# Attention weights divided by one engine per batch: GpSimd for the first, VectorE for the second

## The chip, the cores and the metric

The kernel runs on one core of one Trainium2 chip. The metric is the device time of one launch in microseconds (us). A profile records one execution: every instruction of the five engines, with its start and length, and the DMA transfers. The engines are called here as the profile calls them or by name: PE is TensorE (matrix products; PEld its loading of weights), DVE is VectorE, ACT is ScalarE, POOL is GpSimd, and SP issues DMAs.

## The reference

Attention over a narrow window feeds two gated blocks. Cut to what matters here:

```python
# q, k, v: (2 batches, 8 heads, 768 positions, 64); n_global 8, n_local 96
scores = scale * q @ k.T + bias             # bias falls with the distance
scores = where(is_global | is_local, scores, -1e9)
a = exp(scores - max(scores, -1))
a = a / (sum(a, -1) + 1e-9)                 # the division that the change is about
x = a @ v                                   # -> (2, 768, 512)
x = (sigmoid(conv5(x)) * (x @ w_val)) @ w_out
h = relu(x @ w_in)
out = (h * sigmoid(conv3(h))) @ w_out2
```

## The kernel before

**Tiles.** A batch of 768 positions is six tiles of 128; the twelve tiles are numbered t = 0 to 11, so 0 to 5 are the first batch. Since the window is narrow, a tile of queries meets only its own tile of keys and the one before it: its scores are 128x256 for each of the eight heads (128x128 in tiles 0 and 6, the first of a batch).

**A tile in `fast_attention`.** It goes in two halves of four heads. TensorE makes the scores (L461). For each head VectorE adds the bias and finds the row's extreme in one custom instruction (`least`, L472, reads the scores from PSUM), and ScalarE takes the exponential and its row sum (`grow`, L477). When four heads are there, GpSimd adds 1e-9 to the four sums (`guard`, L488) and VectorE takes the reciprocals (`invert`, L491). Then each head's weights are multiplied by its reciprocal, in place in SBUF: this is the division. `on_dve` (L498) does it on VectorE, `on_pool` (L501) on GpSimd. TensorE then transposes two heads at a time (L528), ScalarE or VectorE copies the result out of PSUM (L532, L538), and TensorE multiplies it with the values (L553). The weights stand in a ring of 11 buffers `p`.

**Beside it.** The weight matrices come in units of 128x512 as 64-bit numbers, and each unit is made into float32 by ScalarE (L262), GpSimd (L264) and twice VectorE (L269, L272: a pair). `w_out` and `w_in` are multiplied with one another beforehand: 32 products of 128x512 on TensorE (L319), whose results VectorE and ScalarE split into two parts `W` (L236, L234). The taps of the convolutions are VectorE's (L671), with a first one on ScalarE or GpSimd (L666, L667). After this the kernel is a long row of TensorE products in three passes (L243 to L245); the first of them, the "values" of the first half of batch 0 with the matrix `w_val` (`wv` in the rows), need all four units of `wv`.

**The order.** Nothing is scheduled while the chip runs except by each engine's own queue, which is worked off in order. A planner (`Plan`) lays out all steps when the kernel is built: each step has an engine, an estimated cost and what it depends on, and the planner emits them by the resulting order. A step with two ways (`POOL=` or `DVE=` beside its engine) goes to the engine that would finish it first by the planner's estimates; so did the divisions.

Of the kernel before, what the change touches and what calls it, by code (L numbers as in the profile page):

```python
# [36 lines left out]
BIG = NEG * 2.0 ** NH * 1.01  # L37
QKSCALE = 1.0 / math.sqrt(D)
XPAIRS = 2
RAWS, MBUFS, HBUFS, Z2BUFS, PBUFS, PTBUFS, KQBUFS, VBUFS = 3, 2, 6, 3, 11, 4, 3, 4  # L40
EARLY = -5.0
LANDING = 2.4
# [40 lines left out]
class Plan:  # L83

    LAG = {"PE": 0.2, "ACT": 0.15, "DVE": 0.15, "POOL": 0.15, "SP": 0.0}
    START = {"DVE": 0.4, "ACT": 1.2, "SP": 0.3}
# [122 lines left out]
def act_us(n, sbuf=True, scaled=False, sums=False):  # L211
    return 0.05 + 0.000834 * n + 0.042 * sbuf + 0.092 * scaled + 0.093 * sums


def dve_us(n, scaled=False):
    return 0.069 + 0.001042 * n + 0.061 * scaled
# [6 lines left out]
def pool_us(n):  # L223
    return 0.17 + 0.0013 * n
# [27 lines left out]
def to_f32(c, dst, raw, n, bufs, reads, token):  # L252
# [5 lines left out]
    def whole(): return high().bitcast(F32)  # L258
    def bits(): return dst().bitcast(I32)
# [3 lines left out]
    pl.add(  # L263
        "POOL", pool_us(n), lambda: nc.gpsimd.tensor_scalar(whole(), whole(), 0.0, 1.0, ALU.mult, ALU.mult),  # L264
        bufs, reads + [token], [tail],
# [113 lines left out]
def head_ways(c, n, out, d, h):  # L379

    nc, k = c.nc, -slope(h) / QKSCALE
    return {
        "POOL": (0.02 + pool_us(n), lambda: nc.gpsimd.tensor_scalar(out(), d, k, 1.0, ALU.mult, ALU.mult)),
        "ACT": (act_us(n), lambda: nc.scalar.activation(out(), d, AF.Copy, scale=k)),
# [24 lines left out]
def fast_attention(c, ap):  # L409

    nc, ident, pl = c.nc, c.ident, c.plan
# [29 lines left out]
    def held(d, ts):  # L441
        return [d[t] for t in ts if t in d]

    for t in range(nt):
# [4 lines left out]
        nk = len(js) * P  # L449
        st, p = sts.new(), {}  # L450
        load(t)
        for half in range(2):
# [40 lines left out]
            four = [("p", t, h) for h in range(4 * half, 4 * half + 4)]  # L493
            pl.add("POOL", 0.12, guard, [st], four, [("r", t, half)])
            pl.add("DVE", 0.2, invert, [st], [], [("r", t, half)])
            for h in range(4 * half, 4 * half + 4):
                def on_dve(h=h, st=st, w=p[h], nk=nk):
                    nc.vector.tensor_scalar(w.t[:, :nk], w.t[:, :nk], st.t[:, 2, h : h + 1], None, ALU.mult)  # L498

                def on_pool(h=h, st=st, w=p[h], nk=nk):  # L500
                    nc.gpsimd.tensor_scalar(w.t[:, :nk], w.t[:, :nk], st.t[:, 2, h : h + 1], 1.0, ALU.mult, ALU.mult)  # L501

                pl.add(
                    "DVE", 0.13 + 0.00052 * nk, on_dve, [p[h], st], [("r", t, half)], [("p", t, h)],
                    POOL=(0.1 + pool_us(nk), on_pool),
                )

        def first_keys(t=t, i=i):
            r = (c.first[0] if t == 0 else kq[t].t)[:, :, 0, 0:GW]
# [3 lines left out]
        if i == 0:  # L513
            pl.add("POOL", 0.4, first_keys, held(kq, [t]), [("kq", t)], ["gl"])
        elif i < NT - 1:
            pl.add("POOL", 0.4, first_keys, held(kq, [t]), ["gl"], [("kq", t)])

        xp = c.ring["x"].new()
        pts = {}
        for pr in range(NPAIR):  # L520
# [15 lines left out]
            def by_dve(pt=pt, w=pts[pr], nw=len(js)):  # L536
# [5 lines left out]
                DVE=(dve_us(2 * nk), by_dve),  # L542
            )

            if pr % XPAIRS < XPAIRS - 1:
                continue

            def output(prs=range(pr - XPAIRS + 1, pr + 1), pts=pts, xp=xp, js=js):
                o = xp.t.rearrange("p (a q) -> p a q", q=P)
                for pr in prs:  # L550
                    for n, j in enumerate(js):
                        for z in range(2):
                            nc.tensor.matmul(  # L553
                                o[z * D : (z + 1) * D, pr, :], vals(j, 2 * pr + z), pts[pr].t[:, z, n, :],
                                start=n == 0, stop=n == len(js) - 1,
                            )

            prs = range(pr - XPAIRS + 1, pr + 1)
            pl.add(
                "PE", 0.213 * len(js) * XPAIRS, output, [xp] + [pts[q] for q in prs] + held(vs, js),  # L560
                [("pts", t, q) for q in prs] + [("v", j) for j in js], [("xp", t, q) for q in prs], mode="x",
            )
        if 0 < i < NT - 1:
# [10 lines left out]
            DVE=(  # L574
                dve_us(512),
                lambda xp=xp, i=i: nc.vector.tensor_copy(
                    c.x[:, :, XP + i * P : XP + (i + 1) * P], xp.t.rearrange("p (a q) -> p a q", q=P)
                ),
            ),
# [252 lines left out]
def attention_gated_mlps(ctx, tc, kq, v, nn, w_val, conv_w, w_out, w_in2, w_out2, out):  # L832
# [41 lines left out]
    def arm(fast):  # L874
        with ExitStack() as es:
# [42 lines left out]
            if fast:  # L918
                masks(c, ap)
                attention = fast_attention(c, ap)  # L920
                next(attention)
                n0 = len(pl.work)
# [78 lines left out]
```

## Time and profile before

| | |
|---|---|
| median of 3 runs | 289.19 us (288.85 to 289.6) |
| the profiled execution | 289.12 us |
| its span, first to last instruction | 286.9 us |
| mean granted TensorE clock | 0.998 |
| busy: PE, DVE, ACT, POOL | 94%, 83%, 65%, 33% |

The span is 2.2 us shorter than the time that the execution itself took. Busy shares are means over the whole span; they say little of a kernel that has stages with different limits, so the rows further below are taken by stretch. The lengths of instructions that follow one another on an engine overlap by some 0.08 us in the records, so what an instruction costs its queue is its record less that overlap (net).

### The profile page before, as it was taken

What the parts mean: (1) busy time and instruction counts of PE and PEld (TensorE: products, weight loads), DVE (VectorE), ACT (ScalarE), POOL (GpSimd) and SP (SyncE); (2) the same over time, 40 slices, a digit from 0 to 9 for tenths busy, and PEclk for the clock granted to TensorE, in tenths of its full rate; (3) what the DMA queues carried; (4) which work ended last, traced back from release to release, by engine and by line L of the source; (5) the groups of instructions that cost most, each with busy time, mean ns of one, the idle gap of its engine ahead of it and who ended that gap; (6) DMA issues with size and microseconds to landing.
All of it is one profiled execution on the core that took longest, in us unless ns stands there. A gap on an engine that the chain in (4) does not pass through costs nothing.

```text
span 286.9 us, 5416 instructions
## 1 busy us (share of the span) xinstructions
PE 270.1 (94%) x1832; PEld 227.9 (79%) x1832; DVE 238.6 (83%) x607; ACT 187.2 (65%) x468; POOL 95.4 (33%) x208
## 2 busy tenths in 40 slices
PE   2689799999999999999999999999999999999993
PEld 2567556564557998999999999988999988899882
DVE  3899999999999999999899999999985654356600
ACT  2899798967677879775688554894464354445510
POOL 4555557445554405563443310320512000003000
PEclk9999999999999999999999999999999999999999
DMA  4985756645634111023510000010000011000112
GB/s 133 344 322 143 239 197 213 251 138 169 216 108 148 48 65 58 9 75 93 170 43 0 2 0 0 1 39 38 37 2 0 0 73 39 37 0 2 39 73 85
DMA packets 10276, 26.17 MB, mean 91 GB/s; under 512 B 1408, under 2 KB 2688, under 8 KB 10240
## 3 DMA queue, kind: packets, MB, share of 16 engines
q1 hardware_dynamic: 9440, 25.22, 26.3%
q10 hardware_dynamic: 800, 0.52, 0.6%
q8 instruction: 16, 0.26, 0.4%
q14 instruction: 20, 0.16, 0.2%
HBM read 22.59 MB, written 3.15 MB: 90 GB/s over the span
## 4 chain that ended last, share of the span: by engine, by line
PE 73%; DVE 15%; POOL 3%; issue 3%; ACT 3%; POOLq 1%; DVEq 0%; ACTq 0%
PE s L244 8%; PE s L245 8%; PE s L243 8%; PE f L243 7%; PE f L245 7%; PE f L244 7%; PE s L461 4%; PE x L553 4%; PE t L528 4%; DVE p L472 3%; DVE z L671 2%; PE t L243 2%; PE t L245 2%; PE x L245 2%; PE x L244 2%
## 5 line engine op out<-in xcount | busy, mean ns | idle before, releaser
L477 ACT ACTIVATE p<-p,st 128x256 f32<-128x256 f32 (+1 forms) x96 | 46.1, 483 | 8.0 <-DVE st L472 6.4
L671 DVE SCALAR_TENSOR_TENSOR z<-h,cw,z 128x384 f32<-128x384 f32 x64 | 39.9, 630 | 12.6 <-ACT z L666 10.9
L673 ACT ACTIVATE z<-z 128x384 f32<-128x384 f32 (+2 forms) x48 | 25.2, 524 | 26.2 <-DVE z L671 25.5
L671 DVE SCALAR_TENSOR_TENSOR z<-x,cw,z 128x400 f32<-128x400 f32 (+1 forms) x64 | 39.6, 643 | 0.2
L244 PE MATMUL s<-w,g 128*128 128x512 f32 (+1 forms) x104 | 39.2, 377 | 0.0
L245 PE MATMUL s<-w,g 128*128 128x512 f32 (+1 forms) x104 | 39.2, 377 | 0.0
L243 PE MATMUL s<-w,g 128*128 128x512 f32 (+1 forms) x104 | 39.1, 376 | 0.0
L501 POOL TENSOR_SCALAR p<-p,st 128x256 f32<-128x256 f32 (+1 forms) x50 | 32.5, 660 | 11.0 <-DVE st L491 8.7
L528 PEld LDWEIGHTS t<-ident,p 128*128 128x128 f32 x176 | 19.8, 141 | 16.6 <-issue 5.0
L528 PE MATMUL t<-ident,p 128*128 128x128 f32 x176 | 28.7, 282 | 4.1 <-ACT pts L532 2.1
L319 PE MATMUL f<-w,w 128*128 128x512 f32 x64 | 30.8, 602 | 0.0
L472 DVE CUSTOM_DVE_ANT_0 p<-s,B 128x256 f32<-128x256 f32 x80 | 30.5, 410 | 0.0
L243 PE MATMUL f<-gg,Wh 128*128 128x400 f32 (+1 forms) x80 | 27.7, 347 | 0.0
L245 PE MATMUL f<-gg,Wl 128*128 128x400 f32 (+1 forms) x80 | 27.0, 338 | 0.0
L244 PE MATMUL f<-gg,Wh 128*128 128x400 f32 (+1 forms) x80 | 27.0, 338 | 0.0
L461 PE MATMUL s<-kq 64*128 64x128 f32 x320 | 25.7, 292 | 0.8 <-DVE st L472 0.7
L461 PEld LDWEIGHTS s<-kq 64*128 64x128 f32 x320 | 21.5, 194 | 4.9 <-issue 2.6
L667 POOL TENSOR_SCALAR z<-h,cw 128x384 f32<-128x384 f32 x10 | 8.9, 887 | 45.9 <-DVE z L671 31.0
L264 POOL TENSOR_SCALAR raw<-raw 128x512 f32<-128x512 f32 x24 | 18.3, 764 | 16.7 <-ACT m L262 14.1
L236 DVE TENSOR_TENSOR g<-z,g 128x384 fp32r<-128x384 f32 x32 | 17.8, 562 | 5.9 <-ACT g L234 5.9
L245 PEld LDWEIGHTS s<-w,g 128*128 128x128 f32 x104 | 19.5, 188 | 3.8
L244 PEld LDWEIGHTS s<-w,g 128*128 128x128 f32 x104 | 19.6, 188 | 2.8
(117 smaller groups left out, 633.6 us busy)
## 6 DMA issues: line engine op xcount, KB each, us to landing
raw<-in_moe_w_out_dram SPq DMA_DIRECT2D x12, 512.0 KB, 3.4
kq<-in_kq_dram SPq DMA_DIRECT2D x11, 512.0 KB, 4.4
raw<-in_moe_w_in_dram SPq DMA_DIRECT2D x8, 512.0 KB, 5.3
v<-in_v_dram SPq DMA_DIRECT2D x11, 256.0 KB, 3.6
out_dram<-o SPq DMA_DIRECT2D x11, 256.0 KB, 2.0
raw<-in_moe_w_val_dram SPq DMA_DIRECT2D x4, 512.0 KB, 3.5
v<-in_v_dram SPq DMA_DIRECT2D x8, 64.0 KB, 2.8
x<-in_kq_dram ACTq DMA_DIRECT2D x1, 256.0 KB, 4.0
```

The source lines that it names most:

```text
L243: nc.tensor.matmul(out, lh, rh, start=first, stop=False)
L244: nc.tensor.matmul(out, lh, rl, start=False, stop=False)
L245: nc.tensor.matmul(out, ll, rh, start=False, stop=last)
L264: "POOL", pool_us(n), lambda: nc.gpsimd.tensor_scalar(whole(), whole(), 0.0, 1.0, ALU.mult, ALU.mult),
L319: nc.tensor.matmul(ps.t, big["wot"].t.bitcast(F32)[:, e, cs], big[wi].t.bitcast(F32)[:, e, :], start=e == 0, stop=e == 3)
L461: nc.tensor.matmul(out, keys(t0, pr, 1)[hs], keys(j, pr, 0)[hs], start=True, stop=True)
L472: nc.vector.tensor_tensor_reduce(w.t[:, :nk], sc, bias, -QKSCALE, 3.0e38, ALU.add, ALU.min, st.t[:, 0, h : h + 1])
L477: nc.scalar.activation(w.t[:, :nk], w.t[:, :nk], AF.Exp, bias=st.t[:, 0, h : h + 1], scale=-1.0, accum_out=st.t[:, 1, h : h + 1],)
L501: nc.gpsimd.tensor_scalar(w.t[:, :nk], w.t[:, :nk], st.t[:, 2, h : h + 1], 1.0, ALU.mult, ALU.mult)
L528: nc.tensor.transpose(o[:, z, n, :], p[2 * pr + z].t[:, n * P : (n + 1) * P], ident)
L671: nc.vector.scalar_tensor_tensor(z(), src(k), w()[:, k : k + 1], z(), ALU.mult, ALU.add)
L673: pl.add("ACT", act_us(n), lambda: nc.scalar.activation(z(), z(), AF.Tanh, scale=0.5), bufs, [], [token])
```

## The change

In the first batch (t below `SHARED` = 6) every division is GpSimd's, in the second every one VectorE's; before, the planner placed each by itself. The planner's estimate for GpSimd differs a little from before.

```diff
+SHARED = 6
...
-                pl.add(
-                    "DVE", 0.13 + 0.00052 * nk, on_dve, [p[h], st], [("r", t, half)], [("p", t, h)],
-                    POOL=(0.1 + pool_us(nk), on_pool),
-                )
+                e, us, fn = ("POOL", 0.25 + 0.00094 * nk, on_pool) if t < SHARED else ("DVE", 0.13 + 0.00052 * nk, on_dve)
+                pl.add(e, us, fn, [p[h], st], [("r", t, half)], [("p", t, h)])
```

In the program before, VectorE had 27 of the first batch's 48 divisions and 19 of the second's; GpSimd had 21 and 29. Since the planner lays everything out anew, other steps move too: of the copies out of PSUM VectorE has 14 in place of 19 (L538, L576), and GpSimd makes 12 first taps in place of 18 (L667), ScalarE the rest. Lines above 502 are one lower in the changed kernel, lines from 40 to 500 one higher.

GpSimd's queue in the first batch, around tile 1, before. `st_325` holds the sums of tile 1, `p_` are buffers of weights, L488 is `guard`, L501 the division, L264 a unit of a weight matrix, L511 a copy of the global keys:

```order
L488 TENSOR_SCALAR st_325<-st_325 128x4
L501 TENSOR_SCALAR p_324<-p_324,st_325 128x256
L501 TENSOR_SCALAR p_347<-p_347,st_325 128x256
L264 TENSOR_SCALAR raw_330<-raw_330 128x512
L488 TENSOR_SCALAR st_325<-st_325 128x4
L511 TENSOR_SCALAR kq_305<-gl_225 128x4x32
L264 TENSOR_SCALAR cwr_226<-cwr_226 128x44
L501 TENSOR_SCALAR p_355<-p_355,st_325 128x256
```

The same place now, where `st_318` holds the sums of tile 1:

```order
L489 TENSOR_SCALAR st_318<-st_318 128x4
L502 TENSOR_SCALAR p_335<-p_335,st_318 128x256
L502 TENSOR_SCALAR p_317<-p_317,st_318 128x256
L502 TENSOR_SCALAR p_344<-p_344,st_318 128x256
L502 TENSOR_SCALAR p_339<-p_339,st_318 128x256
L489 TENSOR_SCALAR st_318<-st_318 128x4
L510 TENSOR_SCALAR kq_305<-gl_225 128x4x32
L265 TENSOR_SCALAR raw_270<-raw_270 128x512
L502 TENSOR_SCALAR p_357<-p_357,st_318 128x256
L502 TENSOR_SCALAR p_350<-p_350,st_318 128x256
L502 TENSOR_SCALAR p_388<-p_388,st_318 128x256
L502 TENSOR_SCALAR p_363<-p_363,st_318 128x256
```

Tile 1 had three divisions here and has eight, and the second `guard` stands behind the first four of them. Up to the last reciprocal of tile 5 GpSimd's queue has 42 divisions in place of 19 (8 of 128 columns and 34 of 256, for 4 and 15), 6 units of weight matrices in place of 9, and 2 first taps in place of 3.

VectorE's queue in the first batch, behind a reciprocal of tile 4 (`st_621`), before; `st_754` and `p_772`, `p_788` belong to tile 5, and the second L472 of each pair only writes out the extreme:

```order
L491 RECIPROCAL st_621<-st_621 128x4
L472 ISA p_772,st_754<-s_710,B_223 128x256
L472 ISA st_754 128x1
L498 TENSOR_SCALAR p_727<-p_727,st_621 128x256
L472 ISA p_788,st_754<-s_709,B_223 128x256
L472 ISA st_754 128x1
L498 TENSOR_SCALAR p_749<-p_749,st_621 128x256
L272 SCALAR_TENSOR_TENSOR w8_637<-w8_637,raw_680 128x4x128
```

Now, behind the same reciprocal (`st_612`; tile 5 has `st_761`):

```order
L492 RECIPROCAL st_612<-st_612 128x4
L473 ISA p_760,st_761<-s_732,B_223 128x256
L473 ISA st_761 128x1
L473 ISA p_772,st_761<-s_733,B_223 128x256
L473 ISA st_761 128x1
L473 ISA p_777,st_761<-s_732,B_223 128x256
L473 ISA st_761 128x1
L473 ISA p_780,st_761<-s_733,B_223 128x256
```

The divisions between the score instructions are gone. Up to the last reciprocal of tile 5 VectorE's queue loses 25 divisions (21 of 256 columns, 4 of 128), three L269, two L272 and two taps, and gets two copies out of PSUM of 512 columns, one of tile 1's output and one multiple of the mask more; the L269, L272 and taps now stand behind it. From there to the last unit of `wv` that VectorE finishes there are now 11 divisions of 256 columns and 8 of 128, where there were 3 and 4, also two score instructions of 256 columns and one of 128 more, and two copies of 256 columns less. ScalarE's queue up to tile 5's last exponential has 69 steps in place of 79.

TensorE's queue where the products of the two weight matrices begin (L319), before:

```order
L461 MATMUL s<-kq 128x128 x8
L319 MATMUL f<-w_328,w_637 128x512
L528 MATMUL t<-ident,p 128x128 x4
L319 MATMUL f<-w_328,w_637 128x512 x2
L528 MATMUL t<-ident,p 128x128 x4
L319 MATMUL f<-w_328,w_637 128x512
L553 MATMUL x<-pts,v 64x128 x16
```

Now:

```order
L552 MATMUL x<-pts,v 64x128 x8
L527 MATMUL t<-ident,p 128x128 x4
L320 MATMUL f<-w_415,w_748 128x512 x2
L527 MATMUL t<-ident,p 128x128 x4
L320 MATMUL f<-w_415,w_748 128x512 x2
L527 MATMUL t<-ident,p 128x128 x4
L552 MATMUL x<-pts,v 64x128 x8
```

They began between the transposes of tile 3 and now begin between those of tiles 4 and 5. Behind the second transposes of tile 5 (two heads, four blocks) stand 28 of the 32 products, where there were 22, and one half of tile 4's output product. Between that place and the first product with `wv` there are further the second half of the scores of tile 9 and one more group of four transposes, of tile 8; before, these stood behind the first product with `wv`.

## Rows read from the trace of the kernel before

**Rows 1.** The page's busy time, share of the span, instructions of each engine.

```profile
PE 270.1 (94%) x1832; PEld 227.9 (79%) x1832; DVE 238.6 (83%) x607; ACT 187.2 (65%) x468; POOL 95.4 (33%) x208
```

**Rows 2.** Busy us of PE, PEld, DVE, ACT, POOL in three stretches; then clock, DMA.

```profile
8.70:51.80 43.10, 39.18 (x368) 28.78 (x368) 41.93 (x160) 38.14 (x121) 25.05 (x51) 1.00 0.73 245
51.80:90.80 39.00, 37.63 (x256) 22.00 (x256) 38.61 (x101) 28.32 (x77) 20.88 (x31) 1.00 0.53 172
93.40:282.00 188.60, 188.60 (x1158) 173.08 (x1156) 151.10 (x315) 114.67 (x253) 45.85 (x109) 1.00 0.11 37
```

**Rows 3.** The chain that ended last: start us, us, what; each matmul recorded twice.

```profile
39.39 1.72 PE f L319 x4
...
95.78 0.44 PE t L528 x4
...
104.05 1.09 PE s L461 x16
105.14 1.02 PE x L553 x16
```

**Rows 4.** VectorE's timeline: start us, us, instruction.

```profile
16.84 0.34 DVE L498 TENSOR_SCALAR p<-p,st 128x256 f32<-128x256 f32 x1
...
51.85 0.17 DVE L491 RECIPROCAL st<-st 128x4 f32<-128x4 f32 x1
...
90.16 0.68 DVE L236 TENSOR_TENSOR wvl<-m,wvh 128x512 fp32r<-128x512 f32 x1
```

**Rows 5.** TensorE's timeline.

```profile
55.99 0.60 PE L528 MATMUL t<-ident,p 128*128 128x128 f32 x4
...
93.36 0.43 PE L243 MATMUL f<-gx,wvh 128*128 128x400 f32 x1
```

**Rows 6.** GpSimd by line, 9 to 52 us: busy us, mean ns; idle before.

```profile
L501 POOL TENSOR_SCALAR p<-p,st 128x256 f32<-128x256 f32 x15 | 8.2, 556 | 4.0 <-DVE st L491 3.8
L264 POOL TENSOR_SCALAR raw<-raw 128x512 f32<-128x512 f32 x9 | 6.5, 725 | 2.0 <-ACT w L262 1.9
L488 POOL TENSOR_SCALAR st<-st 128x4 f32<-128x4 f32 x11 | 3.4, 312 | 3.9 <-ACT p L477 3.3
L667 POOL TENSOR_SCALAR z<-x,cw 128x400 f32<-128x400 f32 x3 | 2.6, 888 | 1.3 <-ACT x L570 1.2
L501 POOL TENSOR_SCALAR p<-p,st 128x128 f32<-128x128 f32 x4 | 1.6, 396 | 0.3 <-PE s L461 0.3
L511 POOL TENSOR_SCALAR kq<-gl 128x128 f32<-128x128 f32 x4 | 1.2, 299 | 5.1 <-PE s L461 3.9 <-issue 1.1
```

**Rows 7.** The same, 52 to 91 us.

```profile
L501 POOL TENSOR_SCALAR p<-p,st 128x256 f32<-128x256 f32 x13 | 11.5, 901 | 1.7 <-DVE st L491 1.7
```

**Rows 8.** VectorE by line, 9 to 52 us.

```profile
L498 DVE TENSOR_SCALAR p<-p,st 128x256 f32<-128x256 f32 x21 | 9.7, 478 | 0.0
L269 DVE SCALAR_TENSOR_TENSOR raw<-raw 128x512 int32<-128x512 int32 x9 | 6.1, 680 | 0.0
L272 DVE SCALAR_TENSOR_TENSOR w<-w,raw 128x512 int32<-128x512 int32 x8 | 5.7, 712 | 0.1
L671 DVE SCALAR_TENSOR_TENSOR z<-x,cw,z 128x400 f32<-128x400 f32 x4 | 2.5, 613 | 0.0
L498 DVE TENSOR_SCALAR p<-p,st 128x128 f32<-128x128 f32 x4 | 1.1, 311 | 0.0
```

**Rows 9.** The same, 52 to 91 us.

```profile
L671 DVE SCALAR_TENSOR_TENSOR z<-x,cw,z 128x400 f32<-128x400 f32 x13 | 9.4, 730 | 0.0
L272 DVE SCALAR_TENSOR_TENSOR m<-m,raw 128x512 int32<-128x512 int32 x4 | 3.6, 889 | 0.1
```

**Rows 10.** GpSimd's timeline: one division, and four in a row.

```profile
29.22 0.48 POOL L501 TENSOR_SCALAR p<-p,st 128x256 f32<-128x256 f32 x1 [0.73 <-DVE st L491]
...
83.70 4.96 POOL L501 TENSOR_SCALAR p<-p,st 128x256 f32<-128x256 f32 x4 [0.38 <-DVE st L491]
```

**Rows 11.** The page's costliest groups: GpSimd's divisions over the whole span.

```profile
L501 POOL TENSOR_SCALAR p<-p,st 128x256 f32<-128x256 f32 (+1 forms) x50 | 32.5, 660 | 11.0 <-DVE st L491 8.7
```

## The prediction

> **What bounds the kernel now.** I read the page's busy shares first, then the busy time by stretch, then the chain that ended last. TensorE is busy 94% of the span [rows 1], but that is a mean over two stages. From 93.4 us to 282 us it is busy for all of 188.6 us [rows 2], and the chain runs along it: this stage lasts as long as TensorE's products do, and what VectorE or GpSimd gain within it buys nothing by itself. It can only begin earlier or hold less work. It begins at 93.36 us with the first product with `wv` [rows 5]. Ahead of it, from 8.7 us to 90.8 us, the fullest engine is VectorE: 41.9 of 43.1 us and 38.6 of 39.0 us [rows 2]. VectorE's last subtraction of a unit of `wv` begins at 90.16 us and ends 0.68 us later [rows 4]. So the question is when VectorE and TensorE reach that point. TensorE's own queue is not slack either: it is busy 37.6 of 39.0 us in the second stretch.
>
> I split the first stage at the last reciprocal of tile 5, which VectorE starts at 51.85 us [rows 4]; most of the first batch's attention is then behind it.
>
> **First stretch, VectorE.** A division of 256 columns on VectorE costs its queue 0.26 us undisturbed (0.34 less the overlap of 0.08, [rows 4]), but in this stretch its mean record is 0.478 us [rows 8], so some 0.40 us net of the overlap; of 128 columns 0.23 us (0.311 less 0.08). Removed: 21 x 0.40 + 4 x 0.23 = 9.3 us. Moved behind the reciprocal: three L269 at 0.60, two L272 at 0.63, two taps at 0.53 (net, [rows 8]) = 4.1 us, and one small score instruction, 0.2 us. Added: two copies and tile 1's output at about 0.6 us each and a mask multiple, together some 2.0 us. VectorE's own demand falls by 11.6 us, from 43.1 to about 31.5 us. If nothing else held it, it would reach the reciprocal at 40.3 us.
>
> **First stretch, GpSimd.** It is busy 25.1 of 43.1 us now [rows 2]. In the new order it has, up to the same reciprocal: 34 divisions of 256 columns at 0.55 us (8.2 us for 15) = 18.7; 8 of 128 at 0.40 = 3.2; 12 `guard` at 0.31 = 3.7; 6 units at 0.72 = 4.3; 2 first taps at 0.87 = 1.7; copies of keys and two mask multiples, 2.7 (all from [rows 6] but the last, an estimate by their size). That is 34.3 us. Its queue is in order, and in tiles 1 to 3 the divisions stand directly behind their own `guard`, which must go to VectorE and come back as a reciprocal: about 0.7 us of idle time each (0.73 ahead of the first division in [rows 10]; 3.8 us of such waits in all, [rows 6]). With the first exponentials of tile 1 I take 2.7 us of waits. 8.7 + 34.3 + 2.7 = 45.7 us. VectorE has to wait there for `guard`, so GpSimd sets the end of this stretch: 6.2 us earlier than now, and over 5 us of what VectorE saved are idle. ScalarE is busy 38.1 us of this stretch; with 10 of 79 steps fewer ahead of the last exponential it needs some 33 us and stays just under GpSimd.
>
> The price of GpSimd's division is the doubtful number. Its bounds are 0.48 us, undisturbed [rows 10], and 0.90 us, its mean in the second stretch [rows 7]. I stay at 0.55 us, since the neighbours are the same as now, apart from VectorE's divisions, which are gone from here. That four in a row took 4.96 us at 83.70 [rows 10] shows how far it goes when VectorE's queue has subtractions and taps in it, as at that place. The Trainium skill, SBUF — State Buffer, section "Who interferes with whom", states that VectorE instructions with two SBUF inputs, or in a mode that uses both ports, and GpSimd instructions block each other for a whole instruction, while a VectorE instruction with at most one SBUF input does not interfere; the score instructions read one input from PSUM, so by this the price would go to 0.48 us and the time to some 284.0 us, and the two prices above agree with it.
>
> **Second stretch, VectorE.** It took 39.0 us (51.85 to 90.84). It gets 8 x 0.26 + 4 x 0.23 = 3.0 us of divisions, the 4.1 us moved here, three score instructions, 0.9 us, and loses two copies of 256 columns, 0.7 us: +7.3 us. Against this GpSimd now has 6 divisions here in place of 17. Taps cost 0.730 us here against 0.613 us in the first stretch, L272 0.889 against 0.712 [rows 8, 9]: 13 x 0.12 + 4 x 0.18 = 2.2 us of disturbance, of which I take off 1.5; its 7 own divisions become cheaper by 0.14 us, 1.0 us. Net +4.8 us. Arrival: 45.7 + 39.0 + 4.8 = 89.5 us, against 90.84: 1.3 us earlier.
>
> **Second stretch, TensorE.** The second transposes of tile 5 run at 55.99 us, and 37.4 us later the first product with `wv` starts [rows 5]. They need two divisions that now follow tile 5's last `guard` on GpSimd: 45.7 + 1.1 + 0.2 = 47.0 us, 9.0 us earlier. But between these two places the queue has now 6 more products of the weight matrices at 0.86 us (two in 1.72 us), one more half of an output product, 1.02 us, one half of the scores of a tile, 1.09 us, and four transposes, 0.44 us [rows 3]: 7.7 us more. 47.0 + 37.4 + 7.7 = 92.1 us, 1.3 us earlier than now. This is the later of the two arrivals, so it decides. Behind it, TensorE has 1.09 + 0.44 = 1.5 us less left.
>
> **Behind it.** VectorE's 13 further divisions in tiles 9 to 11 (24 for 11) cost 3.4 us, and it loses four copies of 512 columns and two of outputs, 3.6 us: even. ScalarE gets 5 first taps and most of those copies, some 6 us, beside 114.7 us in 188.6 [rows 2]. I cost both at nothing: TensorE's full queue hides them. If that cover were gone, ScalarE's share would cost at most 6 us.
>
> **Sum.** -1.3 - 1.5 = -2.8 us against the profiled execution's own 289.12 us, 0.07 us under the median of the runs: 286.3 us.
>
> **Rivals.**
> - *GpSimd does not hold VectorE* (division at 0.48 us and no waits for reciprocals): the first stretch ends at some 41 us, VectorE arrives 6 us earlier, TensorE 6 us at most. 289.1 - 6 - 1.5 = about 282 us. For it: VectorE's 31.5 us. Against it: the waits in [rows 6].
> - *No change*: TensorE's products of weights, which begin later now, also wait for the converted units, which stand later in VectorE's queue: with 2 us of idle time more in TensorE's second stretch, where it has 1.4 us now (39.0 less 37.6, [rows 2]), most of the 2.8 us is gone, 289 us. For it: TensorE's 96% in that stretch; against it: that VectorE arrives earlier as well.
> - *Slower: GpSimd becomes the bound of the first stretch.* Every 0.1 us on its division delays tile 5 by 3.4 us. At 0.63 us (286.3 + 34 x 0.08) the gain is gone; at 0.66 us, the mean over all its 50 divisions now [rows 11], the end is 290 us (286.3 + 34 x 0.11), at 0.90 us [rows 7] it would be 298 us (34 x 0.35). For it: the lengths in the second stretch, where VectorE runs instructions with two SBUF inputs; against it: those are less than a third of VectorE's work in the first. The Trainium skill, GPSIMD Engine Reference, section "Engine selection", gives elementwise work to VectorE and calls GpSimd roughly line-rate with one input; the rows (0.48 us against 0.26 us undisturbed) show it slower than that, which is this rival's ground.
>
> **How the numbers follow.** A difference of 0.3%, 0.87 us, is about what a measurement of this kernel can tell from none. My forecast, a gain of 1 to 5 us, has 0.54; the larger gain 0.10; no change 0.15; slower 0.21. Faster 0.64, same 0.15, slower 0.21. The range: the lower end takes in the division at 0.48 us and part of the larger gain, 283.0 us; the upper takes in the division at 0.65 us, 290.6 us. By itself the forecast spans 284.1 to 288.1 us.
>
> **What would show it.** In the profile after: GpSimd busy for 80% or more up to the last reciprocal of tile 5, which stands near 45.7 us; VectorE idle there by some 5 us, waiting for `guard`; GpSimd's division at 0.5 to 0.6 us; VectorE's taps near 0.6 us in the second stretch; the first product with `wv` near 92 us, and no idle time of TensorE behind it. The prediction is wrong if that reciprocal comes after 49 us, if TensorE idles for more than 4 us in its second stretch, or if gaps open on TensorE behind 93 us because VectorE or ScalarE come late.

## The result: slower by 0.9%

| | before | after |
|---|---|---|
| median (20 executions each) | 289.03 us (288.12 to 290.71) | 292.36 us (289.76 to 293.67) |
| ratio, 95% interval | | 1.0092 [1.0067, 1.0117] |
| the profiled execution | 289.12 us | 289.85 us |
| its span | 286.9 us | 287.87 us |
| first product with `wv` starts | 93.36 us | 95.73 us |

The forecast was 286.3 us. The median moved by 3.3 us, the two profiled executions differ by only 0.7 us. The times of each kernel fall on levels: the kernel before has 99 of 161 executions (all sessions of this study) between 288.06 and 289.46 us, with a median of 288.91, and 62 between 289.6 and 290.9, with a median of 290.31. The changed kernel has 12 of 30 between 289.76 and 290.59 (median 289.97), 13 from 292.05 to 292.66 and 5 above 293. So there are two questions: why the lower level rose by 1.06 us where a gain of 2.8 us was forecast, and what the upper levels are. The profile of the changed kernel is of the lower level and answers the first; none of its executions on an upper level was profiled.

The page's line of busy time after the change (answers to [rows 1]), and busy us of PE, PEld, DVE, ACT, POOL by stretch, then clock and DMA (answers to [rows 2]; the first stretch now ends at 48.6 us, the second at 95.3 us):

```profile
PE 268.9 (93%) x1832; PEld 227.0 (79%) x1832; DVE 234.0 (81%) x605; ACT 191.5 (67%) x478; POOL 88.7 (31%) x200
```

```profile
8.70:48.60 39.90, 34.62 (x376) 26.79 (x377) 33.42 (x133) 35.24 (x116) 33.15 (x71) 1.00 0.72 240
48.70:95.30 46.60, 44.45 (x302) 25.95 (x300) 45.23 (x121) 34.33 (x90) 15.09 (x24) 1.00 0.48 156
95.70:283.00 187.30, 187.30 (x1139) 171.96 (x1137) 150.59 (x329) 118.23 (x263) 36.51 (x90) 1.00 0.11 39
```

In the first stretch nobody is full: TensorE 34.6 of 39.9 us, VectorE 33.4, ScalarE 35.2, GpSimd 33.2. Behind 95.7 us TensorE has no gap, as before. VectorE's timeline at the last reciprocal of tile 5 and the last subtraction of a unit of `wv` (answers to [rows 4]):

```profile
48.45 0.18 DVE L492 RECIPROCAL st<-st 128x4 f32<-128x4 f32 x1 [0.90 <-POOL st L489]
...
94.53 0.68 DVE L237 TENSOR_TENSOR wvl<-m,wvh 128x512 fp32r<-128x512 f32 x1
```

TensorE's timeline at the transposes from which the forecast counted, and in front of the first product with `wv` (answers to [rows 5]):

```profile
50.40 0.60 PE L527 MATMUL t<-ident,p 128*128 128x128 f32 x4
...
90.84 0.66 PE L527 MATMUL t<-ident,p 128*128 128x128 f32 x4 [0.34 <-ACT pts L531]
91.42 1.97 PE L552 MATMUL x<-pts,v 128*64 128x128 f32 x32
93.32 2.06 PE L462 MATMUL s<-kq 64*128 64x128 f32 x32
95.31 0.67 PE L527 MATMUL t<-ident,p 128*128 128x128 f32 x4
95.73 0.43 PE L244 MATMUL f<-gx,wvh 128*128 128x400 f32 x1
```

The first product with `wv` waits for nobody: TensorE comes to it out of its own queue, without a gap since 90.84 us. VectorE's last subtraction ended 0.5 us before. So TensorE's queue is the one to account for. It holds the same products in both kernels; the span can change only by the time that they take and by TensorE's idle time. From 24 us to the first product with `wv`, before and after:

```profile
24.00:93.36 69.36, 65.76 (x525) 42.09 (x524) 68.69 (x206) 56.07 (x161) 36.90 (x61) 1.00 0.57 183
```

```profile
24.00:95.73 71.73, 65.70 (x537) 42.16 (x533) 66.56 (x194) 56.56 (x159) 36.81 (x65) 1.00 0.54 176
```

TensorE was idle for 69.36 - 65.76 = 3.6 us and now for 71.73 - 65.70 = 6.0 us: 2.4 us more, at almost the same work. What it waited for there, of the changed kernel (us in total, times, longest), and then of the kernel before:

```profile
PE t L527 <- ACT pts L531: 2.4, 4, 0.8
PE t L527 <- POOL p L502: 1.1, 2, 0.6
PE x L552 <- DMA v<-in_v_dram: 1.0, 1, 1.0
PE t L527 <- DVE pts L537: 0.9, 1, 0.9
PE f L320 <- DVE w L273: 0.5, 1, 0.5
```

```profile
PE t L528 <- ACT pts L532: 1.8, 3, 0.8
PE t L528 <- DVE pts L538: 1.0, 2, 0.6
PE s L461 <- DVE st L472: 0.7, 1, 0.7
```

New are the waits for GpSimd's divisions, for a load of values that a later tile's output needs, and for a converted unit of weights, 2.6 us together. The load is late through TensorE itself: SP's queue waited 1.7 us until an output product (`PE x L552`) had released the buffer. Each wait is short, and the queue behind has no slack to make it good. GpSimd by line from 9 to 48.6 us (answers to [rows 6]):

```profile
L502 POOL TENSOR_SCALAR p<-p,st 128x256 f32<-128x256 f32 x35 | 19.2, 563 | 4.2 <-DVE st L492 3.7 <-PE s L462 0.2
L265 POOL TENSOR_SCALAR raw<-raw 128x512 f32<-128x512 f32 x6 | 4.0, 674 | 0.2 <-ACT w L263 0.2
L502 POOL TENSOR_SCALAR p<-p,st 128x128 f32<-128x128 f32 x8 | 3.1, 408 | 0.3 <-DVE st L492 0.2
L666 POOL TENSOR_SCALAR z<-x,cw 128x400 f32<-128x400 f32 x2 | 2.6, 1280 | 0.0
```

Its divisions cost what was forecast (0.563 us a record). Its waits are 39.9 - 33.15 = 6.75 us in place of 2.7. What VectorE waited for from 9 to 49 us:

```profile
DVE st L492 <- POOL st L489: 1.7, 3, 0.9
DVE pts L537 <- PE t L527: 1.4, 4, 0.6
DVE p L473 <- PE s L462: 1.2, 2, 0.8
DVE p L473 <- PE t L527: 1.2, 2, 0.8
DVE x L575 <- PE x L552: 0.5, 1, 0.5
```

That is 1.7 us for `guard` and 4.3 us for TensorE. From the chain that ended last (`z` L666 is a first tap):

```profile
37.06 1.75 POOL p L502 x2
39.63 1.38 POOL p L502 x3
...
43.65 1.10 POOL z L666
45.36 1.44 POOL z L666
48.96 1.98 POOL p L502 x3
```

Up to 37 us the chain goes round TensorE, VectorE, ScalarE and GpSimd. From 37.06 to 54.6 us it stays on GpSimd's queue but for 0.5 us, and from there to 89.2 us on VectorE's; through ScalarE it comes to TensorE's transposes at 90.84 us.

### The profile page after: what moved, and what is told of

Read it like the earlier page. It is cut to its first block, busy times and chain, and to the rows that moved or that the text cites. A ratio compares the mean times of both kernels' runs of the same rounds, so it can differ in the third digit from the quotient of the medians.

```text
span 287.9 us, 5450 instructions
## 1 busy us (share of the span) xinstructions
PE 268.9 (93%) x1832; PEld 227.0 (79%) x1832; DVE 234.0 (81%) x605; ACT 191.5 (67%) x478; POOL 88.7 (31%) x200
## 4 chain that ended last, share of the span: by engine, by line
PE 72%; DVE 12%; POOL 6%; issue 3%; ACT 2%; SPq 1%; DMA 1%; DVEq 0%; POOLq 0%; ACTq 0%
PE s L245 8%; PE s L246 8%; PE s L244 8%; PE f L244 8%; PE f L246 7%; PE f L245 7%; PE s L462 5%; PE x L552 4%; PE t L527 4%; POOL p L502 4%; DVE p L473 3%; PE t L246 2%; PE x L246 2%; PE x L244 2%; PE t L244 2%
## 5 line engine op out<-in xcount | busy, mean ns | idle before, releaser
L478 ACT ACTIVATE p<-p,st 128x256 f32<-128x256 f32 (+1 forms) x96 | 46.1, 482 | 11.9 <-DVE st L473 10.8
L245 PE MATMUL s<-w,g 128*128 128x512 f32 (+1 forms) x104 | 39.2, 377 | 0.0
L246 PE MATMUL s<-w,g 128*128 128x512 f32 (+1 forms) x104 | 39.2, 377 | 0.0
L670 DVE SCALAR_TENSOR_TENSOR z<-x,cw,z 128x400 f32<-128x400 f32 (+1 forms) x64 | 38.5, 643 | 0.0
L320 PE MATMUL f<-w,w 128*128 128x512 f32 x64 | 30.1, 597 | 0.6 <-DVE w L273 0.5
L265 POOL TENSOR_SCALAR raw<-raw 128x512 f32<-128x512 f32 x24 | 20.6, 859 | 25.4 <-ACT m L263 13.1
L502 POOL TENSOR_SCALAR p<-p,st 128x256 f32<-128x256 f32 (+1 forms) x48 | 26.4, 565 | 4.5 <-DVE st L492 3.9
L531 ACT ACTIVATE pts<-t 128x512 f32<-128x512 f32 (+1 forms) x36 | 20.4, 567 | 5.1 <-PE t L527 4.5
L462 PE MATMUL s<-kq 64*128 64x128 f32 x320 | 23.7, 287 | 0.0
L462 PEld LDWEIGHTS s<-kq 64*128 64x128 f32 x320 | 20.2, 192 | 4.0 <-issue 3.7
L246 PEld LDWEIGHTS s<-w,g 128*128 128x128 f32 x104 | 19.5, 188 | 3.8
L552 PE MATMUL x<-pts,v 128*64 128x128 f32 x320 | 21.5, 277 | 1.0 <-DMA v<-in_v_dram 1.0
L237 DVE TENSOR_TENSOR g<-z,g 128x384 fp32r<-128x384 f32 x32 | 17.4, 551 | 5.9 <-ACT g L235 5.9
```

What stands on the lines that cost most here:

```text
L245: nc.tensor.matmul(out, lh, rl, start=False, stop=False)
L246: nc.tensor.matmul(out, ll, rh, start=False, stop=last)
L320: nc.tensor.matmul(ps.t, big["wot"].t.bitcast(F32)[:, e, cs], big[wi].t.bitcast(F32)[:, e, :], start=e == 0, stop=e == 3)
L462: nc.tensor.matmul(out, keys(t0, pr, 1)[hs], keys(j, pr, 0)[hs], start=True, stop=True)
L478: nc.scalar.activation(w.t[:, :nk], w.t[:, :nk], AF.Exp, bias=st.t[:, 0, h : h + 1], scale=-1.0, accum_out=st.t[:, 1, h : h + 1],)
L552: nc.tensor.matmul(o[z * D : (z + 1) * D, pr, :], vals(j, 2 * pr + z), pts[pr].t[:, z, n, :], start=n == 0, stop=n == len(js) - 1,)
```

## The experiments

"Lower level" below is the median of the lower group of times.

### The halves, and the planner's estimate

```diff
 # e2: first batch all GpSimd, second by the planner; e3 the reverse
-e, us, fn = ("POOL", ..., on_pool) if t < SHARED else ("DVE", ..., on_dve)
+if t < SHARED: pl.add("POOL", 0.25 + 0.00094 * nk, on_pool, ...)
+else: pl.add("DVE", ..., on_dve, ..., POOL=(0.1 + pool_us(nk), on_pool))
 # e4: every division by the planner, with GpSimd's estimate of the changed kernel
+pl.add("DVE", ..., on_dve, ..., POOL=(0.25 + 0.00094 * nk, on_pool))
```

The changed kernel again, for comparison: 

> The changed kernel once more, unchanged. Its 20 times stand in groups, near 289.8, 292.4 and 293.5 us, and the profile on hand is of the 289.85 us one, whose span is only 1.0 us over that of before. If the groups are one stage that is stretched in most executions, a profile of a 292 us execution shows where 2.5 us more go: theory A, a transfer that lands later ahead of the first product with wv, so that this product starts at 98 us or later in place of 95.9 us; theory B, instructions of VectorE and GpSimd that block each other in another order in the first batch, so that the last reciprocal of tile 5 comes at 51 us in place of 48.6 us. If the profile is again of a 289.8 us execution, it tells neither.

Measured: 290.56 us (289.82 to 293.51), ratio 1.0072 [1.0040, 1.0104].

The first half of the change: 

> First batch's divisions all on GpSimd, the second's left to the planner as before (28 on GpSimd, 20 on VectorE). Theory 1 (the first batch on GpSimd is what loses: waits between guard, reciprocal and division): last reciprocal of tile 5 near 48.6 us as in the changed kernel, and the time 1 us or more over that of before, 290 to 292 us. Theory 2 (the second batch on VectorE is what loses, 12 more divisions on the engine that sets the second stretch): the first batch's 3.4 us remain a gain, 286 to 288 us.

Measured: 292.24 us (291.33 to 296.97), 1.0101 [1.0068, 1.0135].

The second half: 

> First batch's divisions left to the planner as before (19 on GpSimd, 29 on VectorE), the second's all on VectorE. Theory 1: no loss from this half, 288 to 290 us. Theory 2: VectorE gets 12 more divisions ahead of the first product with wv, some 3.5 us, with nothing saved in the first batch: 291.5 to 293 us.

Measured: 289.25 us (287.78 to 290.10), 0.9990 [0.9967, 1.0012].

The estimate alone: 

> All divisions left to the planner with its two ways, but with GpSimd's cost put as in the changed kernel (0.49 us in place of 0.60 us for 256 columns); 59 divisions on GpSimd in place of 50. Theories 1 and 2 both say that the estimate by itself does little: 288.3 to 290 us. If the time moves by 2 us or more either way, the planner's layout, and not where the divisions run, is worth as much as the change, theory 3.

Measured: 289.69 us (289.13 to 290.79), 1.0012 [0.9992, 1.0032].

The loss comes with the first batch on GpSimd. The second batch on VectorE costs nothing, although it takes away GpSimd's help there, and a new layout by itself moves the time little (e4). In e2's profile (293.58 us) TensorE idles 73.18 - 66.41 = 6.8 us from 24 us to the first product with `wv`, in e3's 67.92 - 63.94 = 4.0 us.

### One place of TensorE's queue

The profile of e2 showed a second thing: TensorE's products took twice as long until 18.2 us, where in the changed kernel's profile they did so until 12.4 us. Both kernels have the first transpose between the two halves of tile 1's scores, the kernel before has it behind them. From here on the planner's order was kept, and single steps were moved or given to another engine in it, so that nothing else changes.

```diff
 order.sort(key=lambda w: self.at[w])
+w = self.work[76]                              # e5: scores of tile 1, second half,
+order.remove(w)                                # ahead of the first transpose (48);
+order.insert(order.index(self.work[48]), w)    # e6: the reverse, in the kernel before
```

> The changed kernel with one step moved on TensorE alone: the first transpose (tile 0, pair 0) stands behind both halves of tile 1's scores, as in the kernel before, and not between them. The other four queues are unchanged. Theory A (the transpose between the halves keeps TensorE at its lower clock for longer in most executions, 18.2 us in place of 12.4 to 12.9 us, worth 2 to 2.5 us, and that makes the times near 292.4 us): all times lie between 289.3 and 290.8 us, median near 290.0 us, within 0.2 to 0.5% of the kernel before. Theory B (the two groups of times come from elsewhere, DMA landing times or other engines): over half of the times stay above 291.5 us, median near 292 us.

Measured: 292.98 us (290.19 to 293.79, 6 executions), 1.0104 [1.0061, 1.0147].

> The kernel before with the reverse move on TensorE alone: the first transpose stands between the two halves of tile 1's scores. The other four queues are unchanged. Theory A: over half of the times rise by 2 to 3 us, to 291 to 292 us, the rest stay near 289 us. Theory B: all stay between 288.1 and 290.7 us, median near 289.1 us.

Measured: 289.47 us (288.81 to 292.11), 1.0011 [0.9985, 1.0038].

The transpose's place has nothing to do with the levels: theory A, as it was put, falls. What remained was that the profiles of executions on an upper level show the late rise.

### Is GpSimd's queue the limit of the first stretch?

```diff
 # e7, first batch: the addition of 1e-9 ahead of the reciprocal, on VectorE
-nc.gpsimd.tensor_scalar(st.t[:, 1, hs], st.t[:, 1, hs], 1.0e-9, 1.0, ALU.add, ALU.mult)
+nc.vector.tensor_scalar(st.t[:, 1, hs], st.t[:, 1, hs], 1.0e-9, None, ALU.add)
 # e8: heads 3 and 7 of tiles 1 to 5
+if 0 < t < SHARED and h % 4 == 3: fn = on_dve
```

> The first kernel of this series (transpose behind both halves of scores) with the 12 additions of 1e-9 of the first batch on VectorE, directly ahead of the reciprocals, at the same places of all queues: GpSimd loses 12 x 0.31 = 3.7 us and the way to VectorE and back, VectorE gets 12 x some 0.1 = 1.2 us. Theory G (GpSimd's queue with its waits for reciprocals sets the end of the first stretch): the last reciprocal of tile 5 comes near 45.5 us in place of 48.6 us, and the first product with wv some 1.5 to 2.5 us earlier than in that kernel, since VectorE's idle time of 6.9 us shrinks; the time is 1.5 to 2.5 us below it, near 288 us. Theory H (VectorE's own work, its waits for ScalarE's exponentials, sets it): that reciprocal stays within 0.7 us of 48.6 us, and the time changes by less than 0.6 us.

Measured: 292.64 us (290.09 to 294.01), 1.0086 [1.0050, 1.0121]; lower level 290.3 us, as e5's 290.2.

> The same first kernel with the divisions of heads 3 and 7 of tiles 1 to 5 on VectorE, at the same places of all queues: GpSimd loses 10 x 0.55 = 5.5 us, VectorE gets 10 x 0.26 to 0.40 = 2.6 to 4.0 us, which fit into the 6.9 us for which it idles up to the last reciprocal of tile 5. Theory G: that reciprocal comes near 45 us, the first product with wv 2 to 3 us earlier, the time 2 to 3 us below that kernel, near 287.5 us. Theory H: it stays near 48.6 us or comes later, and the time rises by 1 to 3 us, by VectorE's added work.

Measured: 291.57 us (288.66 to 292.68), 1.0049 [1.0013, 1.0086]; lower level near 289.0 us.

Theory G said that taking 3.7 and 5.5 us off GpSimd shortens the stretch by some 3 to 4 us, theory H that it does not get shorter. From the second reciprocal of tile 2, where the clock is up in all, to the last of tile 5 it takes 24.6 us in e5 (24.54 to 49.16), 24.0 us in e7 (28.00 to 52.01) and 23.5 us in e8 (26.73 to 50.22): 0.6 and 1.1 us less. Between these places GpSimd was busy 21.4 us in e5, 20.3 in e7 and 19.0 in e8, and idle 3.2, 3.7 and 4.5 us. So 1.1 and 2.5 us of work were gone there, and about half of that came off the stretch: theory G falls, and GpSimd's queue still counts. Theory H holds for e7, whose lower level is that of e5, and falls for e8: 1 to 3 us more were forecast, and the lower level fell by 1.2 us. What the ten divisions give back is seen on TensorE, whose idle time from 24 us to the first product with `wv` is 72.16 - 66.28 = 5.9 us in e5 and 72.86 - 68.22 = 4.6 us in e8:

```profile
24.00:96.86 72.86, 68.22 (x566) 44.24 (x565) 70.46 (x215) 59.05 (x167) 33.95 (x61) 1.00 0.54 176
```

TensorE's own waits for GpSimd's divisions hardly changed (1.4 us in e5, 1.3 in e8); a wait of 0.9 us for a copy by VectorE is gone. So through which hand-over the ten act is not shown.

### Tile 0, and the second stretch

```diff
+if t == 0 and h % 2 == 0: fn = on_dve           # e9, in the changed kernel; also e11, e12
 # e10, in the kernel before
-"DVE", 0.13 + 0.00052 * nk, on_dve, ...
+"DVE", 0.13 + 0.00052 * nk, on_pool if t == 0 else on_dve, ...
+if SHARED <= t < 9 and h % 4 == 3: fn = on_pool # e11, e12
+if 0 < t < SHARED and h % 4 == 3: fn = on_dve   # e12
```

> The changed kernel with the divisions of tile 0's even heads on VectorE, at the same places of all queues (44 of the first batch's 48 stay on GpSimd). Theory S (eight divisions of tile 0 one after the other on GpSimd leave TensorE waiting between its first transposes, from 12.8 to 15 us, and TensorE, if its clock has not risen by then, stays at the lower one until 18 to 22 us): the second transposes come some 0.8 us earlier, most of the times near 292.4 us and all near 293.5 us go, the median falls to 290.0 us, at most 290.8 us. Rival B (where the clock rises has nothing to do with these divisions): the median stays at 292 us or more.

Measured: 291.21 us (289.84 to 292.46), 1.0061 [1.0032, 1.0089]; six executions at 289.84 to 290.45, six at 291.98 to 292.46, none above.

> The kernel before with all eight divisions of tile 0 on GpSimd (four were VectorE's), at the same places of all queues, and nothing else of the change. Theory S: the median rises by 1.5 to 3 us, to 290.6 us or more, and times near 292 us appear. Rival B: the median stays within 0.6 us of 289.1 us, since the rest of the first batch is as before.

Measured: 289.80 us (288.66 to 290.62), 1.0004 [0.9980, 1.0027]; the two levels of the kernel before.

> The first kernel of this series with the divisions of heads 3 and 7 of tiles 6 to 8 (two of 128 columns, four of 256) on GpSimd as well, at the same places of all queues. Theory V (VectorE's full queue in the second stretch decides when the first product with wv starts): from the last reciprocal of tile 5 to the last subtraction of wv it takes 46.6 us in the changed kernel, here 44.8 to 45.5 us (six divisions, 6 x 0.25 = 1.5 us), the first product with wv comes 1 to 1.8 us earlier, the time falls by as much. Theory T (TensorE's own queue decides, or GpSimd's divisions lengthen VectorE's taps by as much as they save): that stretch stays within 0.6 us of 46.6 us, and so does the time.

Measured: 290.48 us (289.79 to 292.61), 1.0059 [1.0033, 1.0085]; levels as e9.

> The kernel with six divisions on GpSimd and, besides, the divisions of heads 3 and 7 of tiles 1 to 5 back on VectorE, at the same places of all queues: every fourth head's division is on the other engine. If the terms add up (1.4 us of the ten, 1 to 1.8 us of the six), the median is near 287.5 us, under the kernel before by 1.5 us; if the first stretch is bound by TensorE's waits from one tile to the next, the ten are worth less than 0.7 us here and the median is that of the kernel with six within 0.7 us.

Measured: 290.18 us (288.51 to 290.83), 1.0002 [0.9978, 1.0026]; five executions at 288.51 to 289.13, seven at 289.98 to 290.83.

Theory S falls: tile 0's divisions neither make nor remove the levels; only the executions above 293 us did not come again in e9, e11 and e12 (36 executions). Six divisions fewer on VectorE in the second stretch bring 0.2 us (first product with `wv` 46.78 us behind the last reciprocal of tile 5 in e11, 46.98 in e9; VectorE's last subtraction 46.2 and 46.5 us behind it), so theory V falls for T. The ten divisions of e12 lower both levels by 1.6 to 1.8 us against e11, where the expectation had 1.4 us or less than 0.7, and make up the whole of the lower level's loss. All other steps of e12 stand in e11's order, so it is these ten divisions that cost. In the chain that ended last, from 8.7 to 55 us, GpSimd's divisions have 10.8 us in the changed kernel, 5.7 in e11, 1.8 in e12 and 3.2 in the kernel before.

### TensorE busy from the start

```diff
+nc.vector.memset(c.warm, 0.0)        # 128x256 of a buffer that is free then
+for _ in range(3): nc.tensor.matmul(spare, c.warm[:, 0:P], c.warm, start=True, stop=True)
 ...
+if t0 == 0 and half == 1:            # behind the scores of tile 0
+    for _ in range(2): nc.tensor.matmul(spare[:, 0:WIN], c.warm[:, 0:P], c.warm, start=True, stop=True)
```

> The kernel before, with five more products on TensorE that nobody reads (128x256 each): three at the very start, two behind the second half of tile 0's scores, where TensorE waits for 2 us. All other steps are unchanged. Theory C (the two levels of time are TensorE's clock, which rises at 12.4 to 13.6 us or at 18 us and later, by how busy TensorE has been): the clock rises before 12 us in all executions, all times lie within 0.8 us of one another, and the median falls under 288.7 us, by the 1.6 us between the levels or more where the clock rises earlier still. Rival L (the levels come from when loads land): two levels as before, 288.7 and 290.3 us, and the median stays near 289.2 us.

Measured: 290.11 us (288.61 to 291.47), 1.0016 [0.9990, 1.0042].

> The changed kernel with the same five products. Theory C: one level, at 289.8 us or lower by what an earlier rise of the clock gives; the difference to the kernel before with the same products is what the change costs at one clock, 1.0 to 1.5 us by the profiles (2.4 us more of TensorE's idle time ahead of the first product with wv, 1.2 us less of its busy time). Rival L: levels near 290, 292.4 and 293.5 us, median near 292 us.

Measured: 289.79 us (289.48 to 292.04), 1.0011 [0.9988, 1.0034].

> The changed kernel with every fourth division of tiles 1 to 8 on the other engine and half of tile 0's on VectorE, with the same five products. Theory C: one level, 1.0 to 1.5 us under the changed kernel with the five products, since TensorE's idle time ahead of the first product with wv is 4.6 us here in place of 6.0 us; within 0.5 us of the kernel before with them. Rival L: two levels as without them, 288.7 and 290.6 us.

Measured: 288.35 us (288.02 to 290.82), 0.9971 [0.9945, 0.9997].

The second half of the change in one more execution, without the five products in spite of the label: 

> The kernel with the planner's choice in the first batch and all divisions of the second batch on VectorE, as it was run before, without the five products, for its levels on this chip: 287.8 to 288.7 us with the clock rising early, 289.1 to 290.1 us with it rising late.

Measured: 289.34 us; its products are slow until 17.4 us, so it is the upper level.

The second half of the change with the five products: 

> The planner's choice in the first batch, all divisions of the second batch on VectorE, and the five products at TensorE's start. If the first batch is what costs: near 288.0 us where the clock stays up (its profile without the products, 288.09 us, had TensorE idle for 4.0 us between 24 us and the first product with wv, in place of 6.0 us in the changed kernel), 0.5 to 1 us under the kernel before with the products (289.0 us) and 1.5 us under the changed kernel with them (289.7 us). If the second batch's half costs as much: near 289.7 us.

Measured: 288.06 us (287.43 to 288.82), 0.9955 [0.9937, 0.9974] against the kernel before, which has no such products.

What differs is read from TensorE's timeline. e3 and e16 are one kernel. In e3's profiled execution (288.09 us) four records of scores take 0.67 us up to 12.1 us, and at 14.02 us x16 take 1.16 us:

```profile
12.09 0.67 PE L462 MATMUL s<-kq 64*128 64x128 f32 x4
12.69 0.44 PE L529 MATMUL t<-ident,p 128*128 128x128 f32 x2
13.65 0.44 PE L529 MATMUL t<-ident,p 128*128 128x128 f32 x2 [0.52 <-DVE pts L539]
14.02 1.16 PE L462 MATMUL s<-kq 64*128 64x128 f32 x16
```

In e16's (289.34 us) the same instructions start at nearly the same times, but x16 take 2.08 us at 14.46 us:

```profile
12.05 0.67 PE L462 MATMUL s<-kq 64*128 64x128 f32 x4
12.64 0.69 PE L529 MATMUL t<-ident,p 128*128 128x128 f32 x2
13.85 0.69 PE L529 MATMUL t<-ident,p 128*128 128x128 f32 x2 [0.52 <-DVE pts L539]
14.46 2.08 PE L462 MATMUL s<-kq 64*128 64x128 f32 x16
```

In e14's, with the five products (`spare`, and `t<-x`), from 10.12 us on:

```profile
1.19 2.93 PE L866 MATMUL spare<-x 128*128 128x256 f32 x6 [1.19 <-DVE one L868]
5.60 2.08 PE L462 MATMUL s<-x 64*128 64x128 f32 x16 [1.49 <-DMA x<-in_kq_dram]
7.62 2.07 PE L466 MATMUL t<-x 128*128 128x256 f32 x4
...
10.12 0.39 PE L462 MATMUL s<-kq 64*128 64x128 f32 x4
```

Half the length is the higher of TensorE's two clocks, 2.4 in place of 1.2 GHz. The column of the granted clock shows 1.00 for these microseconds too, since the traces' record of the clock begins only with the rise (at 12.67 us in e3, 17.35 us in e16): a slow start has to be read from the lengths. Of the profiled executions without the five products, the nine on a lower level (before, after, e1, e3, e4, e5, e6, e9, e11) have the rise between 12.4 and 13.6 us, the six on an upper one (e2, e7, e8, e10, e12, e16) between 17.4 and 21.6 us. What TensorE did before is alike in e3 and e16 to 0.2 us, so the order of the instructions does not decide it by itself. With the products it comes at 9.6 to 10.0 us in e13 to e15 and at 11.9 us in e17, in one profiled execution of each. The executions of the changed kernel above 292 us, 18 of 30, become 1 of 12 (292.04 us, with a mean granted clock of 0.985). The Trainium skill, TensorE: Matmul & The Clock Gate, part 1, says that TensorE begins at the lower clock and is given the higher one only once it has been kept busy; these traces agree (12.4 us at the soonest without the products, 11.9 us at the latest with them).

Theory C's second claim, one level within 0.8 us, holds for the bulk of e14 and e15 but not for e13: in 7 of its 12 executions, and in 3 each of e14 and e15, the mean granted clock of TensorE fell to between 0.983 and 0.994, and these are 0.6 to 2.7 us longer than the medians of the others. Single executions of e1, e2, e5 and e7 and two of e6 have it too. None of these is a profiled one, so where the clock fell is open. Without them the medians are 289.0 us (e13, 5 executions), 289.7 (e14, 9), 288.2 (e15, 9), and 288.1 for e17, which had none (12). e17 ran on another chip than e13 to e15, but the lower level of the kernel before lay between 288.85 and 289.00 us in all six sessions. So e13's median does not come under 288.7 us even so, as theory C had it. At one clock, then, the change costs 0.7 us, its second half alone gains 0.9 us, and so the first half loses 1.6 us by difference; alone, in a layout of its own (e2), it lost more, with no execution under 291.33 us. e15 is 1.5 us under e14, as expected, and 0.8 us under e13, where 0.5 us was the most expected.

## Why the prediction was wrong, step by step

- **GpSimd sets the end of the first stretch, at 45.7 us: wrong, and the step that failed.** The work was right: 33.15 us, forecast 34.3, with the division at 0.563 us, neither at the 0.48 us nor at the dearer prices that were named. The term that was too small is the waits, 6.75 us for 2.7, and the last reciprocal of tile 5 came at 48.6 us. But another figure for the waits would not mend the step, since GpSimd's queue is not the one bound. The chain stays on it only from 37 us on; VectorE waited 1.7 us for `guard` and 4.3 us for TensorE; and e7 and e8 took 1.1 and 2.5 us of work off GpSimd and got about half. The stretch is a ring of hand-overs (scores, extreme, exponential, sum, reciprocal, division, transpose, copy, product) in which no engine is full. That four divisions one behind the other on GpSimd make one of its links longer is argued from the chain; that these divisions cost the time is shown by e12 and, at one clock, by e15. Adding up one engine's work does not show it.
- **VectorE's demand falls by 11.6 us.** It was busy 33.4 us up to the reciprocal, for 41.9 before: 8.5 us less. It idled 6.5 us, more than the 5 us forecast, and not mainly for `guard`. That this idle time would not shorten the kernel in full was said; that none of it would was not.
- **Second stretch, VectorE: +4.8 us; measured +7.8** (from the start of the reciprocal to the end of the last subtraction 95.21 - 48.45 = 46.8 us, for 39.0). Of the 1.5 us of relief counted on for taps and L272 some 1.2 came: 15 taps at 0.702 us in place of 0.730, four L272 on `m` at 0.683 in place of 0.889. But divisions of 256 columns took 0.385 us and of 128 0.367 us a record, where 0.34 and 0.31 were counted on, 1.0 us more over twenty of them, and VectorE idled 1.4 us, for 0.4 before; the rest is spread over smaller terms. This mattered little, since TensorE came 0.5 us later still; but the chain ran along VectorE here, so the two queues were nearly even, as the 0.2 us of e11 also say. The lines (answers to [rows 9]):

```profile
L670 DVE SCALAR_TENSOR_TENSOR z<-x,cw,z 128x400 f32<-128x400 f32 x15 | 10.1, 702 | 0.0
...
L499 DVE TENSOR_SCALAR p<-p,st 128x256 f32<-128x256 f32 x12 | 4.2, 385 | 0.0
...
L273 DVE SCALAR_TENSOR_TENSOR m<-m,raw 128x512 int32<-128x512 int32 x4 | 2.7, 683 | 0.1
...
L499 DVE TENSOR_SCALAR p<-p,st 128x128 f32<-128x128 f32 x8 | 2.7, 367 | 0.1
```

- **Second stretch, TensorE: right.** From the transposes of tile 5 to the first product with `wv` 37.4 + 7.7 = 45.1 us were forecast and 95.73 - 50.40 = 45.3 us measured. These transposes began at 50.40 us in place of 47.0, and that is nearly all of the 3.6 us by which the first product came later than the 92.1 us forecast. Their two divisions do stand behind tile 5's last `guard` (48.22 us on GpSimd), as forecast, and ended at some 49.9 us by the mean of that run of divisions, five in 3.54 us; TensorE, with products of weights up to there, did not wait for them. So both queues came late, within 0.5 us of one another.
- **1.5 us less behind it: right.** 193.54 us from there to the end before, 192.14 after: 1.4 us less. Costing the extra work of VectorE and ScalarE there at nothing held too; TensorE has no gap.
- **The sum.** +2.37 - 1.40 = +0.97 us of span, for -2.8 forecast. A check was to be had from the rows: TensorE was idle for only 43.1 - 39.2 = 3.9 us of the first stretch and 1.4 of the second [rows 2], and its work does not change. A gain of 2.8 us needed more than half of that idle time to go, in an order that puts more hand-overs into the same ring.
- **The remaining 2.3 us of the median** are in no step of the prediction. Between the levels lie 1.4 us before and 2.6 us after, and 18 of 30 executions are on the upper levels in place of 62 of 161. That this is the late rise of TensorE's clock is shown by the fifteen profiles without the five products and by e14, though not by a profile of the changed kernel itself on an upper level. Why the rise comes late more often there is open, as is why it costs more and what the times above 293 us are: the first transposes' place and tile 0's divisions were tried and did not make the levels.
- **The rival that came nearest** by the median was "slower", but by another mechanism than a dear division, which stayed at 0.56 us. By the profiles it was "no change": TensorE idled 46.60 - 44.45 = 2.2 us in its second stretch, 0.8 us more than before, 0.5 us of it for a converted unit.
- **The signs of being wrong** did not show it: the reciprocal came before 49 us, TensorE idled less than 4 us in its second stretch, and no gaps opened behind. Each sign is about a single queue, and the loss is spread over several.

## What to carry to other kernels

When one engine's queue runs without a gap to the end, its work is fixed, and a change can only win its idle time: read that off first, as the upper bound of any gain, and ask of each moved step whether it lengthens a hand-over in front of that queue. An engine with free time is no free resource if what it gives back is waited for: here its busy time was forecast within 4%, and taking ten of its divisions back still gained 1.6 us. Profile more than one execution where the times fall on levels: where TensorE's clock rises late in some of them, a few products that nobody reads, placed where it would idle at the start, may take that away, as they did here for most; the falls of the clock that came with them in 13 of 36 executions are the other side.

## What was not expected of the hardware

TensorE's clock rose at 12.4 to 13.6 us in some executions of one program and at 17 to 22 us in others, in one kernel (e3, e16) with the same instructions at the same times, to 0.2 us, up to there. Giving TensorE products from 1.19 us on moved the rise to 9.6 to 11.9 us, although TensorE then ran at the lower clock for all that time, and the first scores began 0.6 us later (5.60 for 4.97 us). With this start the mean granted clock fell to 0.983 to 0.994 in 13 of 36 executions of e13 to e15 and in none of e17's 12, on another chip; the cause is open.
